# Top-k attention followed by mixture attention: minima back on VectorE, statistics summed by ScalarE, gate rows turned once, two batches' last tokens in one product

## The chip, the cores and the metric

The kernel runs on one core of a Trainium2 chip. The metric is the time in microseconds of one launch, device time, median of the runs. Five engines matter: TensorE (PE; PEld is its weight load), VectorE (DVE), ScalarE (ACT), GpSimd (POOL) and SyncE (SP), which here issues every DMA.

## The reference, cut to what matters

There are 8 batches of 8 heads, 576 tokens, head size 64. The first stage keeps in each row of the scores the 32 greatest and takes a softmax over them:

```
scores = q @ k.T / sqrt(64)
kth    = 32nd greatest of each row of scores
attn   = softmax(where(scores >= kth, scores, -1e9))
x      = attn @ v                       # heads side by side: [8, 576, 512]
```

The second stage routes each token to 2 of 4 experts and adds their causal attention, weighted:

```
w      = softmax over the 2 greatest of x @ w_gate
for e in range(4):
    a   = softmax(causal(q_e @ k_e.T / 8))   # q_e, k_e, v_e = x @ wq[e], wk[e], wv[e]
    out += w[e] * (a @ v_e @ wo[e])
```

## The kernel before, in words

The work of stage one goes by **pairs** of heads, 32 of them (p = 0 to 31, four to a batch). A pair has 9 tiles of 128 query rows by 576 scores (tile 4 is the last 64 rows of both heads). `topk` (L669) takes them in three groups of three. For each tile PE makes the scores in one of three PSUM slots, ACT copies them to `s3` (L693). Then VectorE finds the 32 greatest of each row: `f1` (L706) is the elementwise greater of the two halves of the row, 288 wide; the elementwise smaller of the halves goes to `fb`; `f4` (L725 to L732) halves the greater part twice more into `oct`, `cand` and `fl`; `MAX8` and `MATCH_REPLACE8` (L720, L740, L748, L753) draw the 32 out of the pieces. ACT turns the scores and the 32nd value into masks (L805).

The smaller halves in `fb` are made in one of two ways, chosen by `by_sums(p, g)`: in 56 of 96 groups by one VectorE minimum (`f3`, L709); in the 40 others (all groups of pairs 0 to 3, the first group of each later pair) by GpSimd, which adds the halves as integers (`sum3`, L713) and then takes away the greater ones (`dif3`, L717).

`stats` (L830) runs twice a pair, over 5 and over 4 tiles. It subtracts the row maximum from the 32 values (`s1`, VectorE, L847), takes exp of all at once (`s3`, ACT, L855), sums them (`s4`, VectorE, L859), takes the logarithm (`s6`, ACT, L869), turns maxima and logarithms into rows on PE (`s8`, L872), copies those out of PSUM (`s9`, ACT, L875), makes the rounding remainder (`s7`, VectorE, L878), and sends the rows through DRAM into the operands (`s10`, L881, `s11`, L910). `tail` (L916) then makes the transposed scores with masks and row constants on PE, exp on ACT (L999) and the product with v.

Stage two, `moe` (L1029), runs once a batch between the pairs of the next batch. For two expert groups `heads` makes projections, causal scores, exp with row sums (L1294, L1297), transposes (L1305) and the product with the values. The row scale, gate over sum, is spread by GpSimd to 128 x 512 (`c3`, L1345, L1354), turned on PE (`c4`, L1360) and copied by ACT to `sm` (`c5`, L1365); VectorE multiplies it onto the product (`ot`, L1389). `output` splits `ot` in high and low parts (L1404, L1407), multiplies five token tiles by `wo` (`prod`; the fifth uses half of its rows), and evicts (L1425) and stores (L1428) them. The last batch is cut in two phases.

The order of instructions on each engine is written out by a planner, `Plan.order` (L164): it places tasks by given costs, `BIAS` numbers by kind of task and due times (`D_...`), and treats VectorE operations named in `PORT` and GpSimd's as shutting each other out. All engines then run their lists in order. The rings of tiles (three PSUM slots, 16 masks, one `fa`, one `fb`, one `sm`) set how far an engine can run ahead.

Of the kernel before, what the change touches and what calls it, by code (L numbers as in the profile page):

```python
# [268 lines left out]
BIAS = {"again": -1899.0233, "av": 15679.8456, "ava": 10427.2415, "avb": 10771.2458, "avm": 15845.8351,  # L269
        "c1": -1852.8816, "c2": -5127.6329, "c3": -4695.4331, "c4": 10458.7088, "c5": -4374.1926, "cast": 8296.7565,  # L270
        "cast_swap": 12925.9074, "check1": 8250.5086, "check2": 16636.3912, "check3": -4095.8349,
        "clear_bd": -4395.6858, "compare": 10023.8423, "constants": 15476.1844, "copy": -1837.6069,
        "count": 16487.5225, "diag": 12137.5833, "dif3": -5190.67, "dup": 12071.7239, "dup1": -3612.2304,
        "dup2": 11671.2985, "e_stage": -2991.5771, "ev": 11765.8621, "ev1": -2232.0939, "ev2": -4540.1411,
        "evo": -3736.9266, "exp": -1921.0252, "expa": -3795.0558, "expb": 9814.6582, "f1": 15196.8934,
        "f3": 16315.0988, "f4": 11499.0542, "f5": 11305.4464, "g1": 12699.3248, "g10": 16283.2708, "g11": 16142.0381,
        "g2": -2120.841, "g3": 8521.2482, "g4": 12149.1318, "g5": 15475.3926, "g6": -1854.2529, "g7": -4536.5045,
        "g8": 15329.495, "g9": 15626.8312, "high_w": 15303.7358, "keep_w": -3593.1327, "load_": -4949.8723,
        "load_swap": -2942.6467, "load_w": 12304.0427, "load_wt": -4002.2091, "loadv": 13357.6438,
        "low_again": 16152.0663, "low_all": 11973.2157, "low_w": 15697.1933, "m_stage": -4096.2514, "mark": -6017.547,  # L280
        "mask": -994.0752, "neg": -2627.9139, "neg2": -3928.364, "o_stage": -4395.2651, "oh": -2614.4769,
        "ol": -5276.0233, "ot": 13458.9352, "prod": -4093.9324, "proj": 10421.0257, "rep": 12037.6253,
        "s1": 13725.5267, "s10": 10481.2468, "s11": 8705.1036, "s2": -3999.6434, "s3": -4692.8519, "s4": -5299.2972,
        "s6": 12369.9012, "s7": 9859.7844, "s8": -4873.1982, "s9": -5448.0936, "s_stage": 15126.1892,
        "scale_w": 10457.8404, "scores": -5662.1338, "st": 9440.2451, "sta": 15328.12, "stb": -2476.6015,
        "store": 9458.6284, "sub": 14437.2113, "sum3": -3569.3722, "t_stage": -1899.0162, "tails": -4327.306,
        "vproj": -2272.1823, "win": 8403.1073, "xh": 11983.7784, "xl": -2062.3912}
# [1276 lines left out]
```

## Time and profile before

| what | us |
|---|---|
| median of 3 runs | 1191.51 (1189.96 to 1191.84) |
| the profiled execution, own time | 1189.98 |
| its span, first to last instruction | 1188.1 |
| PE busy / PEld busy | 1082.8 / 904.1 |
| DVE busy | 1077.2 |
| ACT busy | 945.4 |
| POOL busy | 506.7 |

Busy time is the time in which at least one instruction of the engine is in flight. On DVE and ACT an instruction begins some 0.1 us before the one ahead of it ends, so the step from one start to the next is what an instruction costs in a full stream. PE's ends are modelled.

### The profile page before, as it was taken

How to read it: one execution, taken by the hardware profiler on the slowest of the kernel's cores; microseconds unless marked ns; L12 is line 12 of the kernel's file. 1: busy time of each engine (PE TensorE's matmuls, PEld its weight loads, DVE VectorE, ACT ScalarE, POOL GpSimd, SP SyncE). 2: the span in 40 equal slices, each digit the busy share in tenths (PEclk: the TensorE clock that was granted, in tenths of full speed). 3: DMA queues.
4: the chain of work that ended last, by engine and by line, in shares of the span. 5: the costliest groups of instructions: out<-in, count | busy, mean ns of one | idle time of the engine just before them, and what ended most of it. 6: DMA issues, size and time to landing. Idle time of an engine off the chain costs nothing. (4 is left out here: it accounts for less than half of the span.)

```text
span 1188.1 us, 27980 instructions
## 1 busy us (share of the span) xinstructions
PE 1082.8 (91%) x9234; PEld 904.1 (76%) x9234; DVE 1077.2 (91%) x4383; ACT 945.4 (80%) x1981; POOL 506.7 (43%) x696
## 2 busy tenths in 40 slices
PE   4377779999999999999999999999999999999996
PEld 4266569787887878877887878877897878887885
DVE  7999999999999999999999999999999999988021
ACT  5576777878888897888889897888889887888554
POOL 5676633333553335443543335443543335531112
PEclk7588989999999999999999999999999999999999
DMA  5446433443463444444364344444364344522231
GB/s 134 115 132 216 122 84 107 121 114 98 107 198 99 123 106 140 133 127 103 89 203 114 103 124 143 133 103 126 80 187 121 109 108 131 171 53 62 79 114 43
DMA packets 68585, 141.82 MB, mean 119 GB/s; under 512 B 22856, under 2 KB 26072, under 8 KB 63696
## 3 DMA queue, kind: packets, MB, share of 16 engines
q1 hardware_dynamic: 68432, 139.95, 41.7%
q8 instruction: 75, 1.23, 0.5%
q14 instruction: 78, 0.64, 0.2%
HBM read 67.38 MB, written 14.24 MB: 69 GB/s over the span
## 5 line engine op out<-in xcount | busy, mean ns | idle before, releaser
L805 ACT ACTIVATE mask<-s,top 128x576 bf16<-128x576 f32 x288 | 217.3, 776 | 28.8 <-DVE top L748 28.8
L334 PE MATMUL slot<-opb,opb 128*128 128x320 f32 (+1 forms) x960 | 198.6, 325 | 18.6 <-ACT s L693 7.1
L693 ACT ACTIVATE s<-slot 128x576 f32<-128x576 f32 x288 | 177.9, 647 | 43.9 <-PE slot L334 42.2
L334 PE MATMUL slot<-opa,opa 128*128 128x256 f32 (+4 forms) x984 | 197.3, 320 | 15.6 <-ACT opa L572 6.7
L736 POOL COPY scrap<-cand 128x1 f32<-128x1 f32 x96 | 18.0, 187 | 425.5 <-DVE cand L732 372.0
L999 ACT ACTIVATE pt<-slot 128x576 f32<-128x576 f32 (+2 forms) x297 | 182.1, 648 | 12.9 <-PE slot L334 11.5
L334 PEld LDWEIGHTS slot<-opb,opb 128*128 128x128 f32 x960 | 153.6, 204 | 34.5 <-ACT s L693 9.8
L334 PEld LDWEIGHTS slot<-opa,opa 128*128 128x128 f32 (+2 forms) x984 | 144.2, 187 | 39.1 <-ACT opa L572 6.7
L334 PE MATMUL acc<-pt,vt 128*64 128x320 f32 (+1 forms) x1280 | 168.9, 411 | 0.0
L748 DVE MAX8 top<-cand 128x8 f32<-128x160 f32 x576 | 146.5, 306 | 0.0
L334 PEld LDWEIGHTS acc<-pt,vt 128*64 128x64 f32 x1280 | 86.3, 137 | 55.8 <-issue 4.5
L720 DVE MAX8 cand<-fb 128x8 f32<-128x288 f32 x288 | 121.9, 446 | 2.0 <-POOL fb L717 1.8
L334 PE MATMUL slot<-x,wt 128*128 128x288 f32 (+2 forms) x768 | 118.6, 303 | 0.0
L706 DVE TENSOR_TENSOR fa<-s 128x864 f32<-128x864 f32 x96 | 111.6, 1163 | 2.9 <-ACT s L693 2.9
L334 PE MATMUL slot<-negi,mask 128*128 128x128 bf16 (+3 forms) x1632 | 111.1, 218 | 1.1 <-DVE rows L878 0.5
L334 PEld LDWEIGHTS slot<-x,wt 128*128 128x128 f32 x768 | 107.1, 192 | 1.7 <-issue 0.5
L713 POOL TENSOR_TENSOR fb<-s 128x864 int32<-128x864 int32 x40 | 82.4, 2059 | 41.8 <-ACT s L693 41.8
L785 POOL TENSOR_TENSOR ind<-cand,top 128x486 bf16<-128x486 f32 x96 | 96.3, 1003 | 6.3 <-DVE top L748 5.7
L717 POOL TENSOR_TENSOR fb<-fb,fa 128x864 int32<-128x864 int32 x40 | 87.7, 2193 | 22.9 <-DVE fa L706 22.7
L334 PEld LDWEIGHTS <-mask 128*128 128x128 bf16 (+1 forms) x1632 | 79.8, 102 | 20.4 <-issue 9.6
L748 DVE MAX8 top<-oct 128x8 f32<-128x72 f32 x576 | 93.1, 214 | 0.0
L753 DVE MATCH_REPLACE8 cand<-top,cand 128x160 f32<-128x160 f32 x288 | 85.5, 303 | 0.1
(185 smaller groups left out, 2354.0 us busy)
## 6 DMA issues: line engine op xcount, KB each, us to landing
raw<-in_qk_dram SPq DMA_DIRECT2D x31, 576.0 KB
wt<-kept SPq DMA_DIRECT2D x17, 1024.0 KB
opa<-raw SPq DMA_DIRECT2D x93, 144.0 KB
opb<-raw SPq DMA_DIRECT2D x93, 144.0 KB
vt<-in_vL_dram SPq DMA_DIRECT2D x32, 320.0 KB
opa<-opa SPq DMA_DIRECT2D x62, 144.0 KB
opb<-opb SPq DMA_DIRECT2D x62, 144.0 KB
wt<-keptv SPq DMA_DIRECT2D x8, 1040.0 KB
```

The lines of the kernel that those rows point to most:

```text
L334: nc.tensor.matmul(o, l, r, start=start, stop=stop, skip_group_check=True)
L693: nc.scalar.activation(s3.t[:, n], sl.t[:, o0:o0 + S], AF.Copy)
L706: v.tensor_tensor(out=fa.t, in0=s3.t[:, :, 0:288], in1=s3.t[:, :, 288:576], op=OP.max)
L713: nc.gpsimd.tensor_tensor(out=i(fb.t), in0=i(s3.t[:, :, 0:288]), in1=i(s3.t[:, :, 288:576]), op=OP.add)
L717: nc.gpsimd.tensor_tensor(out=i(fb.t), in0=i(fb.t), in1=i(fa.t), op=OP.subtract)
L720: v.max(out=c.t[:, n, 152:160], in_=fb.t[:, n])
L736: nc.gpsimd.tensor_copy(scrap[:, g:g + 1], c.t[:, 0, 143:144])
L748: v.max(out=w.top.t[0][:, 3 * g + n, 8 * r:8 * r + 8], in_=oc.t[:, n] if r < 2 else c.t[:, n, 0:160])
L753: v.match_replace(out=c.t[:, n, 0:72] if r == 1 else src, in_values=src, imm_value=LOW, in_to_replace=w.top.t[0][:, 3 * g + n, 8 * r:8 * r ...
L785: nc.gpsimd.tensor_tensor(out=ind.t[:, 0:486].rearrange("p (a n) -> p a n", a=3), in0=c.t, in1=m32[:, 3 * g:3 * g + 3, 31:32].to_broadcast ...
L805: nc.scalar.activation(w.mask[j].t, s3.t[:, n], AF.Relu, bias=w.top.t[0][:, 3 * g + n, 31:32], scale=-1.0)
L999: es[j] = add("ACT", act(a1 - a0), lambda sl=sl, pt=pt, o0=o0, a0=a0, a1=a1: nc.scalar.activation(pt.t[:, a0:a1], sl.t[:, o0 + a0:o0 + a1] ...
```

## The change

All minima become VectorE's `f3`; `sum3`, `dif3`, the separate `low_all` and the tile `fl` go, and `f4` writes its minimum into `fa`. `stats` no longer subtracts and sums on VectorE: ACT takes one exp for each tile, with the scaled maximum as bias and the row sum accumulated, 5 or 4 small instructions in place of one; VectorE makes the two scaled maxima. `s7` goes to GpSimd, which cannot read PSUM, so ACT copies the rows twice. The gate rows are multiplied on the narrow tile, turned by one PE transpose, copied (128 columns) and spread over partitions by DMAs through DRAM. The last 64 tokens of an even batch wait in `keep`, and the odd batch multiplies both by `wo` at once, with two stores. The mask ring goes from 16 to 15; all of the planner's `BIAS` and due times have other values.

```diff
-    PORT = ("s1", "f1", "f3", "f4", "ot", "constants", "sub", "low_again")
-    SLACK = 178.3475
+    PORT = ("f1", "f3", "f4", "ot", "constants", "sub", "low_again")
+    SLACK = 147.8033
...
-MP = (16, 9)
-def by_sums(p, g):
-    return p < 4 or g == 0
+MP = (15, 9)
...
-            def sum3(s3=s3, fb=fb):
-                nc.gpsimd.tensor_tensor(out=i(fb.t), in0=i(s3.t[:, :, 0:288]), in1=i(s3.t[:, :, 288:576]), op=OP.add)
-            def dif3(fa=fa, fb=fb):
-                nc.gpsimd.tensor_tensor(out=i(fb.t), in0=i(fb.t), in1=i(fa.t), op=OP.subtract)
...
-                v.tensor_tensor(out=fl.t, in0=l, in1=r, op=OP.min)
+                v.tensor_tensor(out=l, in0=l, in1=r, op=OP.min)
...
-            if by_sums(w.p, g):
-                low_ = add("POOL", pool(864), sum3, cps, bufs=[s3, fb], prio=P0)
-                low_ = add("POOL", pool(864), dif3, [t1, low_], bufs=[fa, fb], prio=P0)
-                t = add("DVE", 1850, f4, [t1], bufs=[fa, fl, c, oc], prio=P0)
-            else:
-                t = low_ = add("DVE", dve(864), f3, cps + [t], bufs=[s3, fb], prio=P0)
+            t = add("DVE", dve(864), f3, cps + [t], bufs=[s3, fb], prio=P0)
+            t = add("DVE", 2706, f4, [t], bufs=[fa, fb, c, oc], prio=P0)
...
         def s1():
-            nc.vector.tensor_tensor(out=parts()[0], in0=m32[:, js], in1=m32[:, js, 0:1].to_broadcast([P, n, TOPK]),
-                                    op=OP.subtract)
-        def s2():
-            g.tensor_scalar(parts()[1][:, 0:n], w.top.t[0][:, js, 0], 0.125, None, op0=OP.mult)
+            v.tensor_scalar(st.t[3][:, 0:n], mx, -0.125, None, op0=OP.mult)
+            v.tensor_scalar(parts()[1][:, 0:n], mx, 0.125, None, op0=OP.mult)
         def s3():
-            nc.scalar.activation(d, d, AF.Exp, scale=0.125)
-        def s4():
-            nc.vector.tensor_reduce(u[:, 0], d, AX.X, OP.add)
+            for i in range(n):
+                nc.scalar.activation(d[:, i], w.top.t[0][:, j0 + i], AF.Exp, scale=0.125, bias=st.t[3][:, i:i + 1],
+                                     accum_out=u[:, 0, i:i + 1])
...
         def s9():
-            nc.scalar.activation(rows.t[0:2 * n, 0], sl.t[0:2 * n, 0:P], AF.Copy)
+            nc.scalar.activation(rows.t[1][0:2 * n], sl.t[0:2 * n, 0:P], AF.Copy)
+            nc.scalar.activation(rows.t[0][0:2 * n, 0], sl.t[0:2 * n, 0:P], AF.Copy)
         def s7():
-            nc.vector.tensor_tensor(out=rows.t[0:2 * n, 1], in0=sl.t[0:2 * n, 0:P], in1=ft(rows.t[0:2 * n, 0]), op=OP.subtract)
+            g.tensor_tensor(out=rows.t[0][0:2 * n, 1], in0=rows.t[1][0:2 * n], in1=ft(rows.t[0][0:2 * n, 0]), op=OP.subtract)
...
             def c3():
+                nc.gpsimd.tensor_tensor(out=su[:, f0:f1], in0=su[:, f0:f1], in1=g[:, f0:f1, 2 * gp:2 * gp + 2], op=OP.mult)
...
             def c4(sl=sl):
-                for t in full:
-                    nc.tensor.transpose(sl.t[:, t * P:(t + 1) * P], sc[:, (t + 1) * P:(t + 2) * P], identf)
-                if ts[-1] == 4:
-                    mm(sl.t[:, 512:S], sc[:, 0:P], id2, start=True, stop=True)
+                nc.tensor.transpose(sl.t[0:gn, 0:P], sm.t[1].rearrange("p t h -> p (t h)")[:, us], identf)
             def c5(sl=sl):
-                nc.scalar.activation(sm.t[2][:, P + c0_:P + c1_], sl.t[:, c0_:c1_], AF.Copy)
+                nc.scalar.activation(gr.t[0:gn], sl.t[0:gn, 0:P], AF.Copy)
+            def c6():
+                nc.sync.dma_start(gd[0:gn], gr.t[0:gn])
+            def c7():
+                for h in range(2):
+                    nc.sync.dma_start(sm.t[2][64 * h:64 * h + 64, f0 * P:f1 * P].rearrange("p (t n) -> p t n", n=P),
+                                      rows[h][None].to_broadcast([64, nf, P]))
+                    if ts[-1] == 4:
+                        nc.sync.dma_start(sm.t[2][64 * h:64 * h + 64, 512:S],
+                                          gd[gn - 1:gn, 64 * h:64 * h + 64].to_broadcast([64, D]))
...
+            if ts[-1] == 4:
+                q = 0 if general else 64 * (b % 2)
+                if not q:
+                    rest[:] = [Buf(KEEP), []]
+                kp, kdeps = rest
+                parts_of_output(512, S, lambda k: kp.t[:, k, q:q + 64], [kp], kdeps)
-            for t in ts:
+            for t in ts if general or b % 2 else ts[:-1] if ts[-1] == 4 else ts:
```

## Rows read from the trace of the kernel before

**Rows 1.** The page: busy time of each engine over the span

```profile
PE 1082.8 (91%) x9234; PEld 904.1 (76%) x9234; DVE 1077.2 (91%) x4383; ACT 945.4 (80%) x1981; POOL 506.7 (43%) x696
```

**Rows 2.** Busy us by stretch: length, PE, PEld, DVE, ACT, POOL, then clock, DMA

```profile
60.00:180.00 120.00, 90.27 (x686) 73.54 (x685) 118.55 (x477) 86.65 (x166) 73.41 (x75) 0.87 0.49 140
...
300.00:1020.00 720.00, 701.64 (x6141) 588.38 (x6137) 706.37 (x2897) 617.58 (x1290) 312.12 (x435) 1.00 0.45 126
...
1080.00:1160.00 80.00, 78.17 (x659) 63.28 (x657) 24.57 (x79) 51.05 (x139) 12.53 (x31) 1.00 0.25 80
```

**Rows 3.** PE's longest total waits, 300 to 1020 us: us, times, longest

```profile
PE slot L1305 <- ACT pr L1294: 4.1, 5, 0.8
```

**Rows 4.** Groups by form, VectorE: busy us, mean ns, idle before and releaser

```profile
L706 DVE TENSOR_TENSOR fa<-s 128x864 f32<-128x864 f32 x96 | 111.6, 1163 | 2.9 <-ACT s L693 2.9
L727 DVE TENSOR_TENSOR fl<-fa 128x432 f32<-128x432 f32 x96 | 82.5, 859 | 0.0
L725 DVE TENSOR_TENSOR cand<-fa 128x432 f32<-128x432 f32 x96 | 73.6, 767 | 1.4 <-DVE fa L706 0.5
L847 DVE TENSOR_TENSOR stat<-top 128x160 f32<-128x160 f32 x32 | 14.3, 446 | 0.0
```

**Rows 5.** VectorE in order of time: start us, duration us, instruction

```profile
502.21 0.31 DVE L847 TENSOR_TENSOR stat<-top 128x160 f32<-128x160 f32 x1
502.43 1.06 DVE L706 TENSOR_TENSOR fa<-s 128x864 f32<-128x864 f32 x1
503.40 0.32 DVE L859 TENSOR_REDUCE stat<-stat 128x5 f32<-128x160 f32 x1
...
504.59 0.61 DVE L725 TENSOR_TENSOR cand<-fa 128x432 f32<-128x432 f32 x1
...
512.63 0.26 DVE L878 TENSOR_TENSOR rows<-slot,rows 10x128 fp32r<-10x128 f32 x1
512.82 0.07 DVE L753 MATCH_VALUE_LOAD cand<-top,cand 128x8 f32 x1
...
516.39 2.46 DVE L727 TENSOR_TENSOR fl<-fa 128x432 f32<-128x432 f32 x1
```

**Rows 6.** GpSimd in order of time: two operations beside which VectorE is slow

```profile
303.78 2.20 POOL L1407 TENSOR_TENSOR qk<-ot,qk 128x576 fp32r<-128x576 f32 x1 [4.19 <-ACT qk L1404]
...
515.90 2.48 POOL L717 TENSOR_TENSOR fb<-fb,fa 128x864 int32<-128x864 int32 x1 [1.60 <-DVE fa L706]
```

**Rows 7.** The same group of VectorE within 0 to 180 us

```profile
L727 DVE TENSOR_TENSOR fl<-fa 128x432 f32<-128x432 f32 x16 | 22.4, 1397 | 0.0
```

**Rows 8.** ScalarE in order of time: small exp with accumulated sum

```profile
1149.25 0.37 ACT L1294 ACTIVATE raw<-slot,cand 128x128 f32<-128x128 f32 x1
...
1149.59 0.38 ACT L1294 ACTIVATE raw<-slot,cand 128x128 f32<-128x128 f32 x1
```

**Rows 9.** Groups by form, ScalarE: busy us, mean ns, idle before and releaser

```profile
L1365 ACT ACTIVATE sm<-slot 128x576 f32<-128x576 f32 x14 | 9.1, 652 | 12.9 <-PE slot L334 12.9
L875 ACT ACTIVATE rows<-slot 10x128 fp32r<-10x128 f32 x32 | 8.4, 261 | 1.4 <-PE slot L872 1.2
```

**Rows 10.** PE in order of time: the gate transposes; two products with `wo`

```profile
528.58 0.60 PE L1360 MATMUL slot<-identf,sm 128*128 128x128 f32 x4
529.02 0.33 PE L334 MATMUL slot<-id,sm 128*128 128x64 f32 x2
...
1108.27 3.03 PE L334 MATMUL slot<-wt,qk 128*128 128x512 f32 x12
```

**Rows 11.** The end in order of time: the last exp, the last gate product

```profile
1163.41 0.22 ACT L1297 ACTIVATION_READ_ACCUMULATOR pr<-slot,sm 128x1 f32 x1
...
1174.53 0.49 DVE L1389 TENSOR_TENSOR ot<-acc,sm 128x320 f32<-128x320 f32 x1 [4.91 <-PE acc L334]
```

**Rows 12.** SyncE's issues in order of time: rows to DRAM, then back

```profile
512.92 0.29 SPq L881 DMA_DIRECT2D rows<-rows  x1
...
515.06 0.28 SPq L910 DMA_DIRECT2D opa<-rows  x1
```

More of the change, by code (lines that the diff above doesn't have):

```diff
@@ L267 @@
 PEF = 1.0
[L269 to L287, printed above, removed]
@@ L312 @@
+D_K2 = 17.91344
+D_PREP = 208.15554
+D_SC = 317.40652
+D_TIE = 423.80842
+D_MASK = -45.9613
+D_STAT = 100.1117
+D_TAIL = -174.2598
+D_STEP = 78.50603
+D_MOE = -37.1532
+D_TAILB = 48.57598
+D_MOEB = -37.6551
+D_LASTB = -17.92233
+D_LAST = 293.25228
+D_PEN = 121.3378
+D_SPAN = 272.97653
+MP = (15, 9)
+D_W = -142.10983
+D_EARLY = 31.89648
 HALVES = (0, 1, 4, 5, 6, 2, 3, 7, 8)
@@ L375 @@
     MASK = ring("mask", [P, S], BF, MP[0])
[L376 to L377 removed]
+    STAT = sets("stat", 2, ([P, 5, TOPK], FT), ([P, 10], FT), ([P, 2, 5], FT), ([P, 5], FT))
+    ROWS = sets("rows", 2, ([10, 2, P], FR), ([10, P], FT))
     PT = ring("pt", [P, S], FT, MP[1])
@@ L902, in stats @@
         t6 = add("ACT", 190, s6, [t], bufs=[st], prio=0)
-        t8 = add("PE", 0, s8, [t2, t6], bufs=[st, sl], prio=0, kind="s8")
-        t9 = add("ACT", act(P), s9, [t8], bufs=[sl, rows], prio=0)
-        t7 = add("DVE", 250, s7, [t9], bufs=[sl, rows], prio=0)
+        t8 = add("PE", 0, s8, [t6], bufs=[st, sl], prio=0, kind="s8")
+        t9 = add("ACT", 2 * act(P), s9, [t8], bufs=[sl, rows], prio=0)
+        t7 = add("POOL", 440, s7, [t9], bufs=[rows], prio=0)
         t = add("SP", dma(1, 4), s10, [t7], bufs=[rows], prio=0, lat=1500)
@@ new lines, in heads, with c4, c5 @@
+            half = "ab"[ph] if final else ""
+            gn = us.stop - us.start
+            gr = Buf(GROWS)
+            def c4(sl=sl):
+                nc.tensor.transpose(sl.t[0:gn, 0:P], sm.t[1].rearrange("p t h -> p (t h)")[:, us], identf)
+            def c5(sl=sl):
+                nc.scalar.activation(gr.t[0:gn], sl.t[0:gn, 0:P], AF.Copy)
+            gd = dr.tile([9, P], FT, name=f"gates{len(kept_gates)}")
+            kept_gates.append(gd)
+            def c6():
+                nc.sync.dma_start(gd[0:gn], gr.t[0:gn])
@@ L1367, in heads @@
             a = add("POOL", 250, c1, exps, bufs=[sm], prio=3)
             a = add("DVE", 125, c2, [a], bufs=[sm], prio=2)
-            a = add("POOL", {"": 1650, "a": 700, "b": 1100}[half], c3, [a, gate], bufs=[sm, gg], prio=3)
-            when(600 * w_ / S)
-            a = add("PE", 0, c4, [a], bufs=[sm, sl], prio=3, kind="c4" + half)
-            scaled = add("ACT", act(w_), c5, [a], bufs=[sm, sl], prio=3)
+            a = add("POOL", 190 if ts[-1] < 4 else 540, c3, [a, gate], bufs=[sm, gg], prio=3)
@@ L1373, in heads @@
+            when(200)
+            a = add("PE", 0, c4, [a], bufs=[sm, sl], prio=3, kind="s8")
+            a = add("ACT", act(P), c5, [a], bufs=[sl, gr], prio=3)
+            a = add("SP", dma(1, 4), c6, [a], bufs=[gr], prio=3, lat=1500)
+            scaled = add("SP", dma(4 if ts[-1] == 4 else 2, 64), c7, [a], bufs=[sm], prio=3, lat=1900)
             acc = Buf(ACC if final and ph else SLOT)
```

161 lines of the change are left out of this document (70 added, 91 removed), and 7 rows, old and new, of the table BIAS.

## The prediction

> **What bounds the kernel now.** The reader looks first at the page, but its shares mislead: DVE and PE are both busy 91% of the span, ACT 80% [rows 1]. The stretches say more [rows 2]. From 60 to 180 us DVE is busy 118.55 of 120 us and PE 90.27: here VectorE's choice of the 32 greatest sets the pace. From 300 to 1020 us DVE has 706.37 of 720 (98.1%) and PE 701.64 (97.4%), ACT 617.58 (85.8%). From 1080 to 1160 us DVE is nearly done (24.57 of 80), and PE, 78.17 of 80, works off what is left. So the kernel has a VectorE head, a long middle in which two engines are full together, and a tail of PE.
>
> Is PE really full in the middle? Its ends are modelled, so a busy time of 97% proves little. The weight loads are the check: 588.38 of 720 in the middle (81.7%) and 63.28 of 80 in the tail (79.1%) [rows 2]. In the tail nothing but PE and its own chain is left; the middle is as dense. And PE's costliest wait there adds up to 4.1 us [rows 3]. I take PE as a bound that stands just behind VectorE. The Trainium skill (Perfetto Trace Analysis, Identifying the Most-Contended Engine) says that matmul busy time is a poor measure and that the share of weight loads tells PE's headroom; by that rule taken alone a fifth of PE would be free in the middle, and VectorE's whole saving would come through: that is the rival "VectorE alone" below. The tail's row speaks against it.
>
> **Minima on VectorE.** Forty groups gain an `f3`. `f1`, of the same shape, steps on by 0.97 us (502.43 to 503.40) [rows 5]: +39 us. What goes with GpSimd's sums is not only GpSimd's time. An undisturbed operation of `f4` at 432 columns takes 0.61 us (504.59); the minimum at 516.39 takes 2.46, while GpSimd's L717 runs from 515.90 for 2.48 us, and ends with it [rows 5, 6]. VectorE stood still until GpSimd was through. Summed by the groups: L727 82.5 - 96 x 0.61 = 24 us, L725 73.6 - 96 x 0.61 = 15, L706 111.6 - 96 x 1.05 = 11, L847 in both forms 2 x (14.3 - 32 x 0.31) = 9: 59 us of standing still [rows 4, 5]. Not all of it leaves: most slow L725 stand beside the output's L1407, 2.20 us at 303.78 [rows 6], which stays. I take 13 us for those and 3 for L706 beside operand work that stays too. So 43 us go, and the minima cost 39 - 43 = -4 us; bounds -20 (all 59 go) to +39 (other GpSimd work takes the place in each case). In the head, where pairs 0 to 3 have 12 of the 40 groups, the exchange is no worse: L727 alone stands still there for 22.4 - 16 x 0.61 = 12.6 us [rows 7], as much as 12 x 0.97 costs, and the stalls of L706, L725 and L847 are gain.
>
> The Trainium skill (SBUF — State Buffer, SBUF: two separate sides) says that VectorE with two SBUF inputs and GpSimd share a port pair as an exclusive lock held for the whole instruction. The rows at 516 us agree, 2.46 against 0.61 us. By the same rule the new `s7` on GpSimd can block VectorE: a rival below.
>
> **Statistics.** VectorE loses, 64 times, a subtraction (step 0.22), a reduction (0.32 less the overlap of 0.09 that L847 and L706 show, 0.23) and the remainder (0.19) [rows 5]; the four-tile forms are shorter, so 0.62 x 64 = 40 us. It gains 128 tiny scalings; the trace has none. They lie between a `MATCH_VALUE_LOAD`, 0.07, and L878, 0.19 [rows 5]: 9 to 24 us, I take 14, nearer the first by size. Net -26. Together VectorE sheds 30 us of 1077.
>
> ScalarE pays. One small exp with accumulator goes from 1149.25 to 1149.59: 0.34 us [rows 8], at 128 columns from PSUM. With 32 columns it is shorter; from L875 to L1365 a column costs (652 - 261)/448 = 0.87 ns [rows 9], so 96 fewer take at most 0.08. I take 0.30 (bounds 0.26 and 0.34): 288 x 0.30 = 86 us. The two old exps, at 128 and 160 columns a little longer than L875's 0.16 in a stream, some 0.20, go: -13. The second `s9` copy adds 64 x 0.16 = 10 (L875's 0.261 [rows 9] less an overlap of 0.1, as on VectorE in [rows 5]). The gate copy shrinks from 0.65 to 0.26 us, 16 times: -6. Four evictions go, each about as long as L1365 less that overlap: -2. Sum +75 us, bounds +60 to +90. In the middle, with 21 of 32 pairs, ACT goes from 617.58 to about 667 of 720, 93%. Its slack of 102 us covers that on average, not at each moment: the five exps of a call are one block of 1.5 us, and the copies that free PE's three PSUM slots queue behind it. I charge 8 us, bounds 0 and 32 (64 blocks x 0.5 us).
>
> **Gate rows and last tokens.** PE loses transposes: four step on in 0.44 us (528.58 to 529.02) [rows 10]. 64 of these and 32 half products (each no more than a transpose) fall to 18: about 64 x 0.11 + 32 x 0.07 - 18 x 0.11 = 7 us. Twelve matmuls of `prod` take 3.03 us [rows 10], so a product 1.5 less overlap, 1.43; four of 40 go: 6 us. PE sheds 13 us of 1083, bounds 8 and 16. GpSimd loses 170 us of sums and most of `c3`; it was no bound.
>
> The new gate path has two DMA trips. One is 2.14 us from the issue at 512.92 to the next that waits for it at 515.06 [rows 12]; issue of `c7`'s four transfers adds about 1 us. At the end, exp is done at 1163.6 and the last `ot` starts at 1174.53 [rows 11]: 11 us, against some 2 for the GpSimd steps and copies and 5.5 for the trips. PE's last product hides it: 0, bounds -1 and +3. In the middle `sm` is held longer, with other pairs' work before it: 0, bound +5 for SyncE, where dups of operands queue behind the wait of `c6`.
>
> **The sum**, against the profiled execution's 1189.98 us. Head: VectorE is the bound, and its saving there is real: 5 pairs x 0.8 us of statistics (26 over 32 pairs) and a third of the stalls outside L727 and L725's L1407, 6 us, -10. Middle and tail: VectorE has -20 left, PE -13; the smaller binds, less the part of both that ends behind a wait. I put -13 for PE, +8 for ACT's blocks: -5. Together -15: 1175. The median of runs stands 1.5 above the profiled execution: 1176 for the median.
>
> **Rivals.**
> - *VectorE alone is the bound.* PE follows into a shorter middle. Then all of -30 comes, and 4 more from a tail with fewer transposes and products: 1191.5 - 34 = 1157. For it: DVE is the fullest engine, 98.1%, and PE sheds work too. Against it: the tail, no denser than the middle [rows 2].
> - *ScalarE's blocks become the bound (slower).* Place: the PSUM slots, in all 64 `s3` blocks. Price: 32 us of PE's waits; against them PE's 13 and 5 of what the head saves: +14, 1205. It decides when PE's waits for ACT in the middle pass 25 us, ACT's share about 96%. For it: PE waits for ACT already in the row that leads the list [rows 3]. Against: the 102 us of slack.
> - *`s7` blocks VectorE.* GpSimd's 64 remainders, each up to 0.45 us (128 columns at L717's 2.48 us for 864 [rows 6] are 0.37, and a start), stop a VectorE operation of two inputs, and more output work falls beside L725: +29 us back on VectorE, the time ends at 1190, no change. For it: the rows at 516 us; against: 0.45 us is short, and most of VectorE's stream reads one input.
> - *The savings hold in part:* the new order leaves more holes at each engine and 5 of 15 us remain: 1186.
>
> **How the numbers follow.** Forecast 1176 (own range 1167 to 1183): 0.36. VectorE alone, 1157: 0.18. In part, 1186: 0.09. No change within 0.2%, what a measurement of this kernel can tell, which `s7` and smaller mishaps share: 0.09. ScalarE's blocks, 1205 (and other losses of the new order): 0.28. So faster 0.63, same 0.09, slower 0.28. Two in ten left out at the ends give 1154 to 1205.
>
> **What would show it.** Right: no L727 over 1 us; L706 + L709 at 96 each with no stall; VectorE busy near 1047; ACT near 1020, 92 to 94% in the middle; PE's weight loads near 82% there; DVE's end some 15 us earlier. Wrong: PE's waits for ACT above 25 us in the middle (blocks), VectorE stalls beside `s7`, waits of `ot` for the gate DMAs, or a tail after VectorE's end that grew by what VectorE saved (then PE alone was the bound).

## The result, and the profile after

The kernel after takes 1178.48 us (median of 4 runs, 1177.11 to 1181.54) against 1191.67 us of the kernel before, here the median of 4 runs. The ratio is 0.9893, 95% interval 0.9869 to 0.9917: 1.1% faster. The forecast was 1176. The profiled execution took 1177.86 us with a span of 1176.0, so 12.1 us of span went.

Line numbers shift: `f1` is now L698, `f3` L701, the two operations of `f4` at 432 columns L708 and L710, the copy of scores L685, the tiny scalings L820 and L821, the small exps L826, the operand remainder on GpSimd L540, the gate DMAs L1332 to L1341, `ot` L1367.

The page's busy times, against [rows 1]:

```profile
PE 1060.4 (90%) x9132; PEld 888.5 (76%) x9132; DVE 1032.9 (88%) x4356; ACT 1006.4 (86%) x2569; POOL 339.9 (29%) x631
```

VectorE is busy 44.3 us less, PE 22.4 less, ScalarE 61.0 more, and the end came only 12.1 us sooner. The same three stretches as in [rows 2], with the same columns (length, PE, PEld, DVE, ACT, POOL, clock, DMA share, GB/s):

```profile
60.00:180.00 120.00, 90.21 (x688) 74.41 (x683) 115.84 (x511) 96.70 (x243) 35.99 (x58) 0.86 0.48 134
300.00:1020.00 720.00, 690.47 (x6049) 582.15 (x6047) 681.32 (x2869) 654.16 (x1679) 225.26 (x403) 0.99 0.47 133
1080.00:1160.00 80.00, 74.47 (x669) 60.82 (x666) 18.33 (x69) 48.30 (x136) 14.87 (x45) 0.98 0.27 86
```

In the middle VectorE falls from 98.1% to 94.6%, PE from 97.4% to 95.9%, ScalarE rises from 85.8% to 90.9%: no engine is as full as VectorE was, and the middle is no shorter. That is read from the starts of `f1`, which open each pair's work on VectorE. From before (L706) and after (L698), start and duration in us:

```profile
207.68 1.05 DVE L706 TENSOR_TENSOR fa<-s 128x864 f32<-128x864 f32 x1
278.18 2.25 DVE L706 TENSOR_TENSOR fa<-s 128x864 f32<-128x864 f32 x1
1022.93 1.05 DVE L706 TENSOR_TENSOR fa<-s 128x864 f32<-128x864 f32 x1
1079.49 1.06 DVE L706 TENSOR_TENSOR fa<-s 128x864 f32<-128x864 f32 x1
```

```profile
194.95 1.06 DVE L698 TENSOR_TENSOR fa<-s 128x864 f32<-128x864 f32 x1 [0.27 <-ACT s L685]
270.04 1.06 DVE L698 TENSOR_TENSOR fa<-s 128x864 f32<-128x864 f32 x1
1014.65 1.06 DVE L698 TENSOR_TENSOR fa<-s 128x864 f32<-128x864 f32 x1 [0.83 <-ACT s L685]
1073.05 1.04 DVE L698 TENSOR_TENSOR fa<-s 128x864 f32<-128x864 f32 x1
```

These are the first `f1` of pairs 6, 8 and 30 and the last of all. The lead over before is 12.7 us at pair 6, 8.1 at pair 8, 8.3 at pair 30 and 6.4 at the last. So the head won 12.7; some 4.6 went between pairs 6 and 8; 22 pairs then ran at the old pace, 744.75 us before and 744.61 after (135.4 a batch); another 1.8 went at the end. From the last `f1` to the end of the span it is 108.6 us before and 102.9 after, 5.7 won. Sum: 12.7 - 6.3 + 5.7 = 12.1.

Groups by form (columns as in [rows 4]; mean in ns):

```profile
L701 DVE TENSOR_TENSOR fb<-s 128x864 f32<-128x864 f32 x96 | 103.3, 1077 | 0.0
L698 DVE TENSOR_TENSOR fa<-s 128x864 f32<-128x864 f32 x96 | 100.9, 1051 | 45.0 <-ACT s L685 44.5
L710 DVE TENSOR_TENSOR fa<-fa 128x432 f32<-128x432 f32 x96 | 65.5, 682 | 0.0
L708 DVE TENSOR_TENSOR cand<-fa 128x432 f32<-128x432 f32 x96 | 57.4, 598 | 0.0
```

The stalls have gone nearly as argued: L727 from 82.5 to 65.5 us (L710), L725 from 73.6 to 57.4 (L708), L706 from 111.6 to 100.9 (L698). But the idle time ahead of `f1` rose from 2.9 us [rows 4] to 45.0, nearly as much as VectorE's work fell. From 300 to 1020 us VectorE works 25.1 us less and waits 29.9 us longer for ScalarE's copies of scores (31.6 against 1.7).

The costliest waits of PE from 300 to 1020 us (us, times, longest), against [rows 3]:

```profile
PE slot L329 <- DMA opa<-raw: 9.5, 5, 3.7
PE slot L329 <- ACT ptm L1280: 5.6, 11, 1.1
PE slot L329 <- ACT pt L966: 4.7, 6, 1.4
PE slot L329 <- ACT pr L1261: 4.3, 5, 1.2
```

What one such wait looks like, some 17 us of it in order of time (idle before and releaser in brackets): VectorE and GpSimd first, then SyncE's issues, PE, ScalarE, and VectorE again.

```profile
389.33 1.04 DVE L698 TENSOR_TENSOR fa<-s 128x864 f32<-128x864 f32 x1
390.30 1.04 DVE L701 TENSOR_TENSOR fb<-s 128x864 f32<-128x864 f32 x1
391.27 0.59 DVE L708 TENSOR_TENSOR cand<-fa 128x432 f32<-128x432 f32 x1
391.79 0.45 DVE L706 MAX8 cand<-fb 128x8 f32<-128x288 f32 x1
392.16 1.45 DVE L710 TENSOR_TENSOR fa<-fa 128x432 f32<-128x432 f32 x1
...
389.26 3.88 POOL L540 TENSOR_TENSOR raw<-raw,opa 128x576 f32<-128x576 f32 x1 [3.48 <-ACT opa L531]
...
391.99 0.35 SPq L1040 DMA_DIRECT2D wt<-keptv  x1
393.16 2.06 SPq L550 DMA_DIRECT2D opa<-raw  x3
...
400.29 2.12 PE L329 MATMUL slot<-opa,opa 128*128 128x256 f32 x8 [3.66 <-DMA opa<-raw]
...
401.49 0.65 ACT L685 ACTIVATE s<-slot 128x576 f32<-128x576 f32 x1 [3.66 <-PE slot L329]
...
406.98 1.06 DVE L698 TENSOR_TENSOR fa<-s 128x864 f32<-128x864 f32 x1 [5.79 <-ACT s L685]
```

Read it from the bottom. VectorE waits 5.79 us for the copies of scores; ScalarE waited 3.66 for the product; PE waited 3.66 for the operand; its transfer was issued at 393.16, when GpSimd's subtraction was through and just behind a load of weights (`wt<-keptv`, 1040 KB, at 391.99). And that subtraction took 3.88 us. No engine is overloaded here; the queues wait in turn.

Such waits are where the lead goes. It falls at five places with a wait of `f1` of 4 us or more: from pair 6 to 7 (12.7 to 8.6 us; the wait ends at 233.22), from 11 to 12 (9.5 to 5.6; the one shown), from 19 to 20 (9.9 to 6.4; 676.45), from 27 to 28 (10.0 to 8.2; 945.72) and from 30 to 31 (8.3 to 6.0; 1051.96). It also falls by 1.4 to 1.9 us at the starts of pairs 10, 18 and 26, each with a wait of 1.4. In between it grows again, most of all from pair 8 to 9, 16 to 17 and 24 to 25 (by 3.5, 4.2 and 4.2 us).

### The profile page after: what moved, and what is told of

Read it like the earlier page. It is cut to its first block, busy times and chain, and to the rows that moved or that the text cites. A ratio compares the mean times of both kernels' runs of the same rounds, so it can differ in the third digit from the quotient of the medians.

```text
span 1176.0 us, 28306 instructions
## 1 busy us (share of the span) xinstructions
PE 1060.4 (90%) x9132; PEld 888.5 (76%) x9132; DVE 1032.9 (88%) x4356; ACT 1006.4 (86%) x2569; POOL 339.9 (29%) x631
## 5 line engine op out<-in xcount | busy, mean ns | idle before, releaser
L777 ACT ACTIVATE mask<-s,top 128x576 bf16<-128x576 f32 x288 | 212.5, 770 | 8.0 <-DVE top L731 8.0
L685 ACT ACTIVATE s<-slot 128x576 f32<-128x576 f32 x288 | 171.8, 647 | 30.4 <-PE slot L329 30.0
L329 PE MATMUL slot<-opb,opb 128*128 128x320 f32 (+1 forms) x960 | 188.6, 318 | 10.0 <-ACT pr L1261 5.0
L329 PEld LDWEIGHTS slot<-opa,opa 128*128 128x128 f32 (+2 forms) x984 | 148.2, 191 | 36.1 <-issue 8.9
L329 PEld LDWEIGHTS slot<-opb,opb 128*128 128x128 f32 x960 | 147.6, 199 | 18.4 <-ACT pr L1261 6.3
L698 DVE TENSOR_TENSOR fa<-s 128x864 f32<-128x864 f32 x96 | 100.9, 1051 | 45.0 <-ACT s L685 44.5
L706 DVE MAX8 cand<-fb 128x8 f32<-128x288 f32 x288 | 129.7, 450 | 0.0
L826 ACT ACTIVATE stat<-top,stat 128x32 f32<-128x32 f32 x288 | 88.8, 317 | 17.6 <-DVE stat L820 17.4
L701 DVE TENSOR_TENSOR fb<-s 128x864 f32<-128x864 f32 x96 | 103.3, 1077 | 0.0
L847 POOL TENSOR_TENSOR rows<-rows,rows 10x128 fp32r<-10x128 f32 x64 | 32.3, 504 | 239.7 <-ACT rows L844 238.8
```

The costliest lines, as they stand in the source:

```text
L329: nc.tensor.matmul(o, l, r, start=start, stop=stop, skip_group_check=True)
L685: nc.scalar.activation(s3.t[:, n], sl.t[:, o0:o0 + S], AF.Copy)
L698: v.tensor_tensor(out=fa.t, in0=s3.t[:, :, 0:288], in1=s3.t[:, :, 288:576], op=OP.max)
L701: v.tensor_tensor(out=fb.t, in0=s3.t[:, :, 0:288], in1=s3.t[:, :, 288:576], op=OP.min)
L706: v.max(out=c.t[:, n, 152:160], in_=fb.t[:, n])
L777: nc.scalar.activation(w.mask[j].t, s3.t[:, n], AF.Relu, bias=w.top.t[0][:, 3 * g + n, 31:32], scale=-1.0)
```

## The experiments

Each row of this table is told below; lead is that over before at pair 6, pair 8, pair 30 and the last `f1`, tail is from the last `f1` to the end of the span.

| kernel | median, us | ratio to before (95%) | lead at 6 / 8 / 30 / last | tail |
|---|---|---|---|---|
| after | 1178.48 | 0.9893 (0.9869 to 0.9917) | 12.7 / 8.1 / 8.3 / 6.4 | 102.9 |
| e1_slack | 1255.17 | 1.0554 (1.0520 to 1.0588) | 11.7 / 12.0 / -37.9 / -38.1 | |
| e2_minima_alone | 1248.61 | 1.0479 (1.0450 to 1.0508) | 5.2 / 9.4 / -46.4 / -50.1 | |
| e3_old_statistics | 1263.85 | 1.0624 (1.0603 to 1.0645) | 4.1 / 9.0 / -32.4 / -43.0 | |
| e4_old_gate_rows | 1238.62 | 1.0425 (1.0401 to 1.0450) | 12.3 / 10.3 / -27.7 / -21.4 | |
| e5_minima_order_kept | 1190.57 | 0.9992 (0.9979 to 1.0005) | 8.4 / 9.7 / -2.5 / -3.2 | 110.0 |
| e6_sums_order_kept | 1265.00 | 1.0624 (1.0603 to 1.0645) | 0.2 / -10.2 / -75.9 / -79.9 | |
| e7_gate_order_kept | 1181.27 | 0.9928 (0.9911 to 0.9945) | 12.7 / 14.0 / 7.5 / 5.0 | 101.8 |
| e8_no_remainder | 1172.23 | 0.9853 (0.9824 to 0.9881) | 13.0 / 10.2 / 15.3 / 13.5 | 101.6 |
| e9_less_scalar | 1175.85 | 0.9885 (0.9866 to 0.9904) | 13.1 / 10.7 / 11.2 / 9.4 | 101.2 |
| e10_less_vector | 1173.56 | 0.9856 (0.9834 to 0.9878) | 14.4 / 11.3 / 9.3 / 7.6 | 102.6 |
| e11_less_pe | 1170.19 | 0.9843 (0.9818 to 0.9868) | 13.1 / 8.5 / 9.4 / 8.2 | 96.0 |
| e12_less_of_three | 1148.66 | 0.9658 (0.9629 to 0.9687) | 19.9 / 16.1 / 28.8 / 29.5 | 96.3 |

Each lead is read from one execution, and executions of one kernel differ by 3 to 13 us (e5's was 4.0 us above its median), so two or three us of lead say little. The kernel before was run again beside each of these, with medians from 1188.19 to 1191.67 us, so small savings are better read from the ratios than from the medians.

### What the order alone is worth (e1_slack)

The kernel after, with one number of the planner changed by 1.5% and the order planned anew; the work is the same.

```diff
-    SLACK = 147.8033
+    SLACK = 150.0
```

> The changed kernel with one number of the planner moved a little (SLACK 147.8 to 150.0), so the same work in a slightly other order. It measures how much a time depends on the order alone. Theory (work on VectorE and PE sets the time): within 4 us of the changed kernel's 1178. Rival (the searched order is what gained): more than 8 us slower, towards 1190.

It took 76.7 us more than after. Its stretch from 300 to 1020 us, and VectorE's wait for scores in it (us, times, longest):

```profile
300.00:1020.00 720.00, 660.42 (x5625) 551.32 (x5626) 632.29 (x2660) 618.95 (x1573) 201.95 (x372) 0.97 0.43 122
```

```profile
DVE fa L698 <- ACT s L685: 62.9, 16, 15.3
```

The lead at pair 6 is nearly the same, 11.7 us; by pair 30 it has turned into 37.9 us lost. VectorE waits twice as long for scores (62.9 us against 31.6 in after), 15.3 at the worst. So the same work in another order costs more than five times what the whole change brought. The rival was right in its direction and far too small. The gain belongs to the change together with its order; whether the old work, in a newly searched order, would gain as much was not tried.

### The parts, planned anew (e2 to e4)

The kernel before with all minima on VectorE; the kernel after with the old statistics; the kernel after with the old gate rows. In each the planner's numbers are those of its parent.

```diff
 def by_sums(p, g):
-    return p < 4 or g == 0
+    return False
```

> The kernel before with all minima on VectorE and nothing else changed. Theory: 39 us of minima against 43 us of standing still, most of the difference in the head: VectorE busy 1077 - 4 = 1073, time 1184 to 1191, no L727 over 1 us. Rival (VectorE's added minima are the cost and the stalls come back beside other GpSimd work): 1200 or more.

```diff
-            v.tensor_scalar(st.t[3][:, 0:n], mx, -0.125, None, op0=OP.mult)
-            v.tensor_scalar(parts()[1][:, 0:n], mx, 0.125, None, op0=OP.mult)
+            nc.vector.tensor_tensor(out=parts()[0], in0=m32[:, js], in1=m32[:, js, 0:1].to_broadcast([P, n, TOPK]),
+                                    op=OP.subtract)
...
-            for i in range(n):
-                nc.scalar.activation(d[:, i], w.top.t[0][:, j0 + i], AF.Exp, scale=0.125, bias=st.t[3][:, i:i + 1],
-                                     accum_out=u[:, 0, i:i + 1])
+            nc.scalar.activation(d, d, AF.Exp, scale=0.125)
...
+            nc.vector.tensor_reduce(u[:, 0], d, AX.X, OP.add)
```

> The changed kernel with the statistics as before (VectorE subtracts, sums and makes the remainder; ScalarE one exp for all tiles). VectorE gains 26 us of work, ScalarE loses about 75. Theory (VectorE bounds the head, PE the middle): the head loses 4 to 6 us, the middle nothing: 1182 to 1187. Rival (ScalarE's blocks hold PE's slots): faster, 1165 to 1173, with PE's waits for ACT in the middle under those of the changed kernel.

```diff
-                nc.tensor.transpose(sl.t[0:gn, 0:P], sm.t[1].rearrange("p t h -> p (t h)")[:, us], identf)
+                for t in full:
+                    nc.tensor.transpose(sl.t[:, t * P:(t + 1) * P], sc[:, (t + 1) * P:(t + 2) * P], identf)
...
-                nc.sync.dma_start(gd[0:gn], gr.t[0:gn])
```

> The changed kernel with the gate rows spread by GpSimd, turned by five PE products and copied in full by ScalarE, as before. Theory (PE bounds middle and tail): PE gains 7 us of work, the tail 1 to 2: 1183 to 1187. Rival (the DMAs of the gate rows hold SyncE's queue and with it the operands of the next pair): faster, 1168 to 1175, and VectorE waits less than 45 us for copies of scores.

All three came out 4 to 6% slower than before, as e1 did without any change of work, and none of the three theories holds. (The rival of the first, 1200 or more, has the number, but e1 comes to it without a single added minimum.) The first also does not give quite the same output, why is not known, so the account does not rest on it. In the head, where the order has had little time to go wrong, they still say something: with the old gate rows the lead at pair 6 is 12.3 us, so the gate edit has no part in it; with the old statistics it is 4.1, with the minima alone 5.2. What happens behind pair 8 cannot be told from the order's part, and nothing on the parts follows from it.

### The parts, in the order that was there (e5 to e7)

So the next three leave the planner's tasks and their order alone and swap the instructions inside them.

```diff
-                nc.gpsimd.tensor_tensor(out=i(fb.t), in0=i(s3.t[:, :, 0:288]), in1=i(s3.t[:, :, 288:576]), op=OP.add)
+                pass
...
-                nc.gpsimd.tensor_tensor(out=i(fb.t), in0=i(fb.t), in1=i(fa.t), op=OP.subtract)
+                v.tensor_tensor(out=fb.t, in0=s3.t[:, :, 0:288], in1=s3.t[:, :, 288:576], op=OP.min)
```

> The kernel before; in the 40 groups of GpSimd's sums the smaller halves come from one VectorE minimum at the place where the second GpSimd operation stood in the order. Every engine's order is else as before (the four kernels ahead were planned anew, and that alone cost 4 to 6%). Theory: +39 us of minima, -43 us of standing still on VectorE; the head, where VectorE is the bound, gains 3 to 6, the middle keeps its period: 1183 to 1189. Rival (the middle's holes depend on when VectorE comes): slower, 1195 or more.

The kernel before with VectorE's minima in the place of `dif3` takes the time of before (0.9979 to 1.0005). VectorE is busy 1080.2 us, 3.0 more than [rows 1]. The 40 new minima cost more than the 0.97 that I took, because the order still puts GpSimd's other work beside them (23 of them take 1.28 to 1.77 us beside its comparison, L783):

```profile
L715 DVE TENSOR_TENSOR fb<-s 128x864 f32<-128x864 f32 x40 | 54.8, 1369 | 0.0
```

In the head, where pairs 0 to 3 have 12 of the 40, the lead at pair 6 is 8.4 us; by pair 30 it is gone. So in the order of before the minima alone give about two thirds of the head's gain, and nothing of it survives the middle. The time lies between the theory's 1183 to 1189 us and the rival's 1195 or more.

```diff
-            for i in range(n):
-                nc.scalar.activation(d[:, i], w.top.t[0][:, j0 + i], AF.Exp, scale=0.125, bias=st.t[3][:, i:i + 1],
-                                     accum_out=u[:, 0, i:i + 1])
+            nc.scalar.activation(d, d, AF.Exp, scale=0.125)
...
+            nc.vector.tensor_reduce(u[:, 0], d, AX.X, OP.add)
             nc.scalar.activation(z[:, n:2 * n], u[:, 0], AF.Ln, bias=eps)
```

> The changed kernel, order kept; the statistics' sums go back: VectorE subtracts and reduces (some 0.4 us more each call, 64 calls, 24 us), ScalarE makes one exp for all tiles of a call (some 70 us less). The remainder stays on GpSimd. Theory (VectorE bounds the head only): the head loses 3 to 5, the middle nothing: 1180 to 1185. Rival 1 (ScalarE bounds the middle): 1150 to 1168. Rival 2 (VectorE bounds all the way): 1195 to 1203.

The kernel after with subtraction, one exp and the reduction back (the reduction directly ahead of the logarithm) has 40.5 us more of VectorE's busy time than after, 66.9 less of ScalarE's, and takes 86.5 us more. Its costliest waits for the statistics from 300 to 1020 us:

```profile
ACT stat L837 <- DVE stat L836: 75.0, 37, 4.1
...
PE slot L840 <- ACT stat L837: 32.6, 24, 2.6
```

ScalarE's logarithm waits 37 times, 2.0 us in the mean, for a sum that stands in VectorE's queue behind other work, and everything behind the logarithm waits too. The price is more than twice the added work. The waits point to the one trip more between two queues in the same task (86.5/64 = 1.35 us a call), but the run does not part the trip from the work. The kernel before had a place for that trip in its order, so this is no price of the statistics edit; it shows what such a trip can cost where the order has no place for it. None of the three expected times holds.

```diff
-                nc.tensor.transpose(sl.t[0:gn, 0:P], sm.t[1].rearrange("p t h -> p (t h)")[:, us], identf)
+                for t in full:
+                    nc.tensor.transpose(sl.t[:, t * P:(t + 1) * P], sc[:, (t + 1) * P:(t + 2) * P], identf)
+                if ts[-1] == 4:
+                    mm(sl.t[:, 512:S], sc[:, 0:P], id2, start=True, stop=True)
...
-                nc.sync.dma_start(gd[0:gn], gr.t[0:gn])
+                pass
```

> The changed kernel, order kept; gate rows spread by GpSimd, turned by five PE products and copied in full by ScalarE as before, no gate DMAs. Theory (PE bounds middle and tail): 5 to 9 us slower, 1183 to 1187. Rival (gate DMAs and SyncE's wait for them hold the next pair's operands): 1165 to 1174.

With the old gate rows in the order of after, the interval (0.9911 to 0.9945) overlaps that of after: by the ratios the gate edit is worth some 4 us, give or take 3.5. The theory's 5 to 9 is not excluded; the rival (1165 to 1174) is. The end shows both sides of it. After, from the copy of the turned gates to the last `ot` (ScalarE, SyncE, PE, VectorE), then the last `ot` of e7:

```profile
1155.21 0.27 ACT L1326 ACTIVATE grows<-slot 5x128 f32<-5x128 f32 x1 [0.72 <-PE slot L1323]
...
1158.59 0.60 SPq L1341 DMA_DIRECT2D sm<-gates  x1
...
1155.98 3.78 PE L329 MATMUL acc<-ptm,v 128*64 128x128 f32 x48 [0.85 <-DVE ot L1367]
...
1161.29 0.49 DVE L1367 TENSOR_TENSOR ot<-acc,sm 128x320 f32<-128x320 f32 x1 [5.46 <-DMA sm<-gates]
```

```profile
1160.65 0.49 DVE L1370 TENSOR_TENSOR ot<-acc,sm 128x320 f32<-128x320 f32 x1 [4.41 <-PE acc L329]
```

In after the last `ot` waits for the DMA, in e7 for PE. After's last `f1` was 1.5 us ahead of e7's, its last `ot` is 0.6 behind: the two DMA trips cost about 2 us at the end.

### One thing less on each engine (e8 to e11)

If one engine or one chain set the middle, taking work off it would shorten the middle. Each kernel is after with the order kept.

```diff
-                else:
+                elif general:
                     nc.gpsimd.tensor_tensor(out=raw.t[:, x], in0=raw.t[:, x], in1=ft(q2[:, c]), op=OP.subtract)
```

> The changed kernel, order kept, without GpSimd's subtraction that makes the low part of q and k (62 operations; the copies by DMA carry the full values in its place, so the scores are others). In the changed kernel one of these took 3.9 us beside VectorE's minima where 1.4 is usual, and PE waited for the operands. Theory (in the middle the chain copy of the operands, subtraction, DMA, scores, copy, first maximum ends last where VectorE waits): VectorE's 45 us of waits ahead of its first maximum fall under 20 and the time by 10 to 20: 1158 to 1168. Rival (PE is full, operands are not what is late): within 4 of 1178.

```diff
-                nc.scalar.activation(ind.t[:, 0:n], ind.t[:, 0:n], AF.Sign, bias=tiny,
-                                     accum_out=signs[:, 3 * w.p + g:3 * w.p + g + 1])
+                pass
```

> The changed kernel, order kept, without ScalarE's 96 counts of the values above the threshold (0.69 us each, 66 us off ScalarE; the result of the count is not used). Which engine bounds the middle is read from this one and the next two, each of which takes some 66 us off one engine. If ScalarE bounds the middle: 1178 - 40 = 1138. If PE or VectorE does: 1174 to 1178. If no single engine does and the in-order chain between them does: 5 to 15 less, 1163 to 1173.

```diff
-                    v.max(out=c.t[:, n, 152:160], in_=fb.t[:, n])
+                    v.max(out=c.t[:, n, 152:160], in_=fb.t[:, n, 0:64])
```

> The changed kernel, order kept; the eight greatest of the smaller halves are taken from 64 columns in place of 288 (288 instructions, 0.23 us less each, 66 us off VectorE; the rest of these halves is not looked at). If VectorE bounds head and middle: 1178 - 60 = 1118. If only the head: 9 to 12 less, 1166 to 1169. If the chain between the engines: 15 to 25 less, 1153 to 1163.

```diff
-                        for x, w in ((xh, wh), (xh, wl), (xl, wh)):
+                        for x, w in ((xh, wh), (xh, wl)):
...
-                        for x, w in ((0, 0), (2, 0), (0, 1)):
+                        for x, w in ((0, 0), (2, 0)):
```

> The changed kernel, order kept; of the three products that make a projection, a value or an output tile only two are made (some 70 us off PE, 15 of it in the tail; the third, the smallest part, is left out). Theory (PE bounds middle and tail): 1178 - 55 to 70 = 1108 to 1123. If VectorE bounds the middle: the tail's 15 only, 1161 to 1165. If the chain between the engines: 1140 to 1160.

The stretch from 300 to 1020 us of e9, e10 and e11, one fence each:

```profile
300.00:1020.00 720.00, 692.28 (x6050) 584.19 (x6049) 680.40 (x2872) 618.41 (x1556) 223.63 (x401) 0.99 0.47 133
```

```profile
300.00:1020.00 720.00, 692.04 (x6030) 585.27 (x6030) 643.22 (x2852) 652.33 (x1677) 216.78 (x401) 0.98 0.47 132
```

```profile
300.00:1020.00 720.00, 659.66 (x5707) 541.07 (x5705) 682.26 (x2871) 649.94 (x1683) 218.71 (x405) 0.98 0.47 133
```

Each edit empties its own engine (ScalarE 654 to 618, VectorE 681 to 643, PE 690 to 660 with weight loads 582 to 541) and leaves those of the other two within some 4 us. The lead from pair 8 to pair 30 moves by +0.5, -2.1 and +0.8 us, against some 30 to 40 us that were taken off. So in the middle neither ScalarE nor VectorE nor PE alone is the bound. e9's median is 2.6 us under that of after, within the interval; e10's 4.9; e11's 8.3; by the ratios they are some 1, 4 and 6. Most of e11's is in the tail (102.9 to 96.0), where less work on PE does shorten the time. e9's time lies where PE or VectorE was to be the bound (1174 to 1178), and the next two speak against both; e10 and e11 gave less than any of their expectations.

e8 tests the wait at 407 us. Its start, GpSimd's subtraction, is left out; the waits of `f1` for scores in the middle did not fall (35.0 us against 31.6), though its lead grew by 5.1 us from pair 8 to 30, and VectorE's busy time fell by 12.3, about what it had stood still beside that subtraction. The theory that the subtraction is the cause of the waits falls: by the ratios leaving it out is worth some 5 us, between the theory's 10 to 20 and the rival's 4. What makes the wait without it stands in e8's rows (SyncE, PE, VectorE):

```profile
387.43 0.35 SPq L1040 DMA_DIRECT2D wt<-keptv  x1
387.82 3.19 SPq L550 DMA_DIRECT2D opa<-raw  x3
...
395.78 2.28 PE L329 MATMUL slot<-opa,opa 128*128 128x256 f32 x8 [3.71 <-DMA rows<-rows]
...
403.04 1.06 DVE L698 TENSOR_TENSOR fa<-s 128x864 f32<-128x864 f32 x1 [6.41 <-ACT s L685]
```

The copies of the operand are again issued right behind the load of weights, which itself goes out 0.04 us after PE's last product with weights (387.39). PE's next product of scores starts 8 us behind the load's issue, released by a transfer (the profile names a small one of 393.08). In between the DMA engines are full. In the kernel after, their busy share from 394 to 400 us is 0.99, the last number but one:

```profile
394.00:400.00 6.00, 2.60 (x39) 2.00 (x35) 5.84 (x34) 3.58 (x10) 3.35 (x6) 1.00 0.99 278
```

In after the load `wt<-keptv` has the copies `opa<-raw` next behind it at 391.99, 661.91 and 930.89 us, and the three longest waits of `f1` in the middle end some 15 us behind each (5.8, 5.0 and 5.6 us). At 518.16 and 787.34 the next copy of an operand is issued over 3 us later, and no wait over 1 us follows within 80 us. In e7 to e12 the three longest waits are at the same three places of the list, with 4.8 to 7.5 us, whichever engine has less to do. In the kernel before, the same load at 394.98 has no copy of an operand next behind it. So these waits belong to SyncE's list, in which a large load stands ahead of copies that are needed soon. That is read from the rows; no run moves the load.

### All three at once (e12_less_of_three)

The edits of e9, e10 and e11 together.

> The last three edits together in the kernel after, its order kept: no counts on ScalarE (about 66 us of it), the last MAX8 of each tile drawn from 64 columns in place of 288 (about 66 us of VectorE), the third product of the two projections and of the output left out (about 70 us of PE). Taken alone they gave 2.6, 4.9 and 8.3 us, and none changed the period of the middle (about 135 us a batch). Theory 'three bounds, one behind the other': each relief alone ran into the next engine; all three at once must shorten the middle by most of the smallest share of the reliefs in it, some 45 us of 720, to a period near 127 us, and the whole to 1115 to 1135 us. Rival 'hand-offs in a fixed order': what paces the middle is waits between queues and what stands in none of the three (transfers, GpSimd, the latency of a round trip); the period stays at 134 to 135 us and the whole at the sum of the three, 1162 to 1170 us.

It took 1148.66 us, 29.8 less than after, where the three alone give 2.6 + 4.9 + 8.3 = 15.8 (by the ratios 28 against 11). Neither expectation holds. The first and last `f1` of the middle and its stretch:

```profile
262.11 1.05 DVE L699 TENSOR_TENSOR fa<-s 128x864 f32<-128x864 f32 x1
...
994.11 1.06 DVE L699 TENSOR_TENSOR fa<-s 128x864 f32<-128x864 f32 x1 [0.83 <-ACT s L686]
```

```profile
300.00:1020.00 720.00, 672.89 (x5841) 554.51 (x5841) 655.75 (x2919) 624.75 (x1579) 218.46 (x403) 0.97 0.48 133
```

The middle from pair 8 to 30 is now 732.0 us, 12.6 shorter than after's 744.6: 133.1 us a batch, 2.3 less, of some 8 that each engine lost (66 us over 8 batches). So the three engines do hold each other: relief of all three shortens the period, by about a quarter of the relief, where that of any one does not. Two at a time were not tried. The rest turns into waits; VectorE's for scores are 39.1 us in the middle, and the three behind the load of weights are still there (6.2, 7.5 and 6.7 us).

A part may be TensorE's clock. The granted clock of the middle, the last number but two of these rows, is 1.00 before [rows 2], 0.99 after and 0.97 in e12: in after it falls at each of the three long waits of PE, for a short stretch, from 2.4 GHz to its lower level, 1.2. There the same eight products take 1.22 us at a granted clock of 1.00 and 2.48 at 0.50, the latter behind a wait of 2.57:

```profile
331.69 1.22 PE L329 MATMUL slot<-opa,opa 128*128 128x256 f32 x8
...
938.10 2.48 PE L329 MATMUL slot<-opa,opa 128*128 128x256 f32 x8 [2.57 <-DMA opa<-raw]
```

By these shares of 720 us PE loses, as an estimate, up to 7 us of work in after and 22 in e12; what that costs in time was not tried. Which of these sets the remaining period stays open.

## Why the prediction came out right, and which step did not hold

- **VectorE's total.** Predicted 1047 us busy, measured 1032.9. Of 59 us of stalls 43 were taken to go; the groups of `f4` and `f1` show 17.0 + 16.2 + 10.7, and the 9 of the old `s1` went with it: 53. The term that was mis-sized is the 13 us of L725 that were to stay beside the output's work: L708, in its place, has a mean of 598 ns, so none stayed. (The reading that the minimum at 516.39 ends with GpSimd's L717 is not exact: it ends 0.47 us behind it, at 518.85.) The scalings were taken as 14 us; in a stream they step on by 0.06 and 0.07 us (0.15 and 0.16 busy), at which 128 of them are 8 us. Start and duration:

```profile
389.20 0.15 DVE L820 TENSOR_SCALAR stat<-top 128x5 f32<-128x5 f32 x1
389.26 0.16 DVE L821 TENSOR_SCALAR stat<-top 128x5 f32<-128x5 f32 x1
```

- **ScalarE's total.** Predicted 1020, measured 1006.4, and 90.9% in the middle against 92 to 94. Of the difference, 6 us are in the copies of scores (177.9 us busy before, 171.8 after) and 5 in the masks (217.3 and 212.5), whose number is the same and whose mean is within 6 ns: they overlap more. The small exp was taken at 0.30 us and is 0.30 from one to the next, of which the accumulator's read is 0.09:

```profile
406.85 0.31 ACT L826 ACTIVATE stat<-top,stat 128x32 f32<-128x32 f32 x1
407.06 0.19 ACT L826 ACTIVATION_READ_ACCUMULATOR stat<-top,stat 128x1 f32 x1
407.15 0.31 ACT L826 ACTIVATE stat<-top,stat 128x32 f32<-128x32 f32 x1
```

  The Trainium skill (ScalarE: Activation LUTs, What ACT_TABLE_LOAD costs) gives an activation whose bias is a pointer operand as about 280 ns and 0.833 ns a column, overlapping the next by some 93. For 32 columns that is an estimate of 0.31 and a step of 0.21; the trace agrees, with 0.31 and 0.21.
- **PE's total.** Predicted -13, measured -22.4 in busy time. Its weight loads are 80.9% in the middle (predicted near 82).
- **The head.** Predicted -10 because VectorE alone is the bound there; measured -12.7 at pair 6. The split came near: 6 for the stalls and 4 for the statistics were predicted, e5 shows 8.4 for the minima alone, which leaves 4.3 by difference. But the relief that e10 gives VectorE moved the lead at pair 6 by 1.7 only, and e12's 7.2: once the change is in, VectorE no longer sets the head alone.
- **The middle: the step that failed.** "The smaller binds" put the gain of middle and tail at PE's 13 us, less 8 for ScalarE's blocks. Measured, the middle gave nothing: 6.3 us of the head's lead were lost between pair 6 and the last `f1`. PE did not set it either: 70 us less on PE (e11) left the period as it was, so taking PE as the bound because the middle "is as dense" as the tail was wrong. What held it is no one engine (e9 to e11): the lead goes at the waits told above, three of the five long ones behind a load of weights in SyncE's list. The prediction has no term for that load; its one term for SyncE, copies behind the wait of `c6`, is not it, since e7 has no such transfers and the same three waits (5.7, 6.1 and 6.7 us). The Trainium skill (Perfetto Trace Analysis, Identifying the Most-Contended Engine) judges PE's headroom by MFU (the matmuls' arithmetic as a share of the peak) and the busy share of weight loads; e11 agrees so far, with 75.1% in the middle and no change of pace. That headroom does not bring VectorE's whole saving, as the rival "VectorE alone" had it (1157): e10 shows that VectorE was no longer the bound either.
- **ScalarE's blocks (the slower rival).** PE's waits for ScalarE in the middle rose from 9.0 to 18.1 us, summed over all their groups, below the 25 named. The 8 us charged has the size of that rise, but e9 shows that ScalarE's load was not its price: 66 us less of it changed nothing that can be told. The blocks of small exps stand in e9 too; e6, which takes them out, adds a trip, so their own price is open.
- **`s7` on GpSimd.** Its 64 operations have a mean of 0.50 us; six of the minima are slow beside one, by 1.6 us in all, so it hardly blocks VectorE (means of `f1` and `f3`: 1051 and 1077 ns). The sign "no L727 over 1 us" failed: 9 of the 96 L710 still take over 1 us, at most 1.47, all beside an operand subtraction, such as the one at 392.16.
- **The gate's DMAs.** 0 was taken, with -1 to +3; about 2 us at the end, hidden in part.
- **The tail.** The sum has no term for it alone; measured -5.7. One product with `wo` fewer stands behind 1073 us (54 matmuls against 60), about 1.5 us by the 3.03 for twelve of [rows 10]. Neither the old gate rows (e7, 101.8) nor the old sums (e6, 103.9) take the gain away. Where the rest comes from is open; the order of the last batch's phases was not tried by itself.

So the total was right in part by luck. Middle and tail together came out at +0.6 us (+6.3 and -5.7) where -5 was forecast, the head at -12.7 where -10 was: two errors that offset each other.

## What to carry to other kernels

Where several engines above 90% run fixed lists against each other, ask of each saving not which engine is fullest but whether any one engine is the bound: take work off each alone, and then off all, before believing in one. Follow a repeated instruction (here the first `f1` of each pair) through both traces; it shows in which stretch a gain comes and where it is given back, which busy shares do not. And when an order is planned by tuned numbers, test parts with the order kept: a new plan of the same work moved the time by 6.5%, nearly six times the effect in question. A wait that comes back at the same place of the list, whichever engine is relieved, belongs to the list: look there for a large load ahead of small transfers that are needed soon.
